# A fused attention and MoE kernel: a head pair's value products come one step later

## The chip, the cores and the metric

The kernel runs on one core of a Trainium2 chip. The metric is the device time in microseconds (us) of one execution. Engines are called as in the profile: PE (matrix products, with PEld for the loading of its weights), DVE (vector), ACT (scalar), POOL (general purpose), SP (issues transfers).

## The reference

```python
scores = scale * q @ k.T + bias          # 4 batches, 8 heads, 768 positions, head size 64
keep = is_global | is_local              # first 8 positions, or the last 96 up to the query
a = softmax(where(keep, scores, -1e9));  attn = a @ v
x = attn as 3072 tokens x 512
h = x @ w_in;  x = (h * cos(h)) @ w_out  # 512 -> 2048 -> 512
# then a top-1 mixture of 8 experts (512 -> 1024 -> 512, relu), skipped for
# tokens with x @ w_skip <= 0; the expert's output is scaled by its gate and added to x
```

All arrays are float32. Each large product is made as three products of split numbers (hi times hi, lo times hi, hi times lo).

## The kernel before, in words

The 3072 tokens are cut into 8 units of 384, that is 3 tiles of 128. A unit goes through attention and then through the first MoE (w_in, cosine, w_out). The two are woven together: while the first MoE works on unit u-1, the attention of unit u is put in between its steps. So the stretch of time of "unit 2" in what follows holds the attention of unit 2 and the MoE of unit 1.

The MoE of a unit has 16 blocks of 128 hidden columns. A block has two steps, and each ends at a slot, 32 slots a unit. In an even slot's step PE makes the 12 products `hp` (L526, input times w_in), in an odd slot's step the products `zp` (L565, activated block times w_out, two blocks behind). Round them stand the other engines' steps of the block: r on DVE (L509, L552), two ACT steps, glo on POOL (L537), and the splitting of the next weights (wi_hi on POOL L483, wi_lo on DVE L492). In unit 0's stretch DVE and POOL also convert the weights (L219, L223, L230, L264), and they are kept after that.

The attention of a unit has 4 head pairs, each 8 slots apart. A pair goes through these functions, and a table says after which slot each is written:

- `att_Tq`, `att_Tk`: transposes of q and k (PE L352, L362).
- `att_S`, once for each of 3 tiles: scores of two heads (PE L396, tile `ps_s`), and for each head one evacuation on DVE (L401) that adds the bias and takes the smallest value. Called S0, S1, S2 here.
- `att_E`: exponentials on ACT (L415), the inverse of the sums on DVE (L419, L420), and six scalings `sc` on POOL (L425).
- `att_P`, for each tile: transposes of the weights (PE L437, L440, tile `ps_p`), copied by ACT to `pT` (L441, L443). Called P0, P1, P2.
- `att_V`: the value products (PE L452, L457, tile `ps_v`). Then ACT rounds the result to `xhi` (L466), and DVE takes the rest, `xlo` (L467), both from `ps_v`. Called V.
- `att_load_va`: the loads of `ld_va`, the values of the tokens before the tile, for the next pair (one buffer).

The rows of the table (s0 is the slot of the pair's first scores; 8 slots later come those of the next pair):

```python
            for t in range(HT):
                at(s0 + t, att_S, u, p, t)
                at(s0 + 5 + t, att_P, u, p, t)
            at(s0 + 9, att_V, u, p)
            at(s0 + 2, att_load_va, u, p)
            at(s0 + 2, att_E, u, p, tail=True)
```

So V of a pair stands at the next pair's slot s0 + 1, behind its S0. The tiles `ps_s`, `ps_p`, `ps_t` and `ps_v` come in turn from one pool of three buffers in PSUM (tag "ps"); a request waits until the tile that had the buffer three requests ago has been read. The requests between two pairs' P2 were S0 (two, one for each head), V, S1 (two), S2 (two), Tq, Tk.

PE and ACT work in the order in which the code is written. On DVE, POOL and SP the order is made by a scheduler when the kernel is built.

DVE has one more kind of work that matters here. From unit 2's stretch on, `logits_v` puts the gate and skip products of an earlier unit on DVE (L623, result `junk` of 128x512, with a small read of its sum behind it): 27 in a unit, two a slot, in slots 4 to 17, so beside the first and second pairs of a unit and not beside the others. Another small piece is `cmin` (L298), a minimum over a block of w_in for a check.

Of the kernel before, what the change touches and what calls it, by code (L numbers as in the profile page):

```python
# [37 lines left out]
def kernel(  # L38
# [7 lines left out]
    NP = H // 2  # L46
# [677 lines left out]
    def at(slot, fn, *a, tail=False):  # L724
        (late if tail else ev).setdefault(slot, []).append((fn, a))
# [6 lines left out]
    for u in range(1, NU):  # L732
        for p in range(NP):
            s0 = HS * (u - 1) + PS * p - 3
            at(s0 - 12, att_load, u, p)
            at(s0 - 5, att_load_v, u, p)
            at(s0 - 5, att_Tq, u, p)
            at(s0 - 4, att_Tk, u, p)
            for t in range(HT):
                at(s0 + t, att_S, u, p, t)  # L740
                at(s0 + 5 + t, att_P, u, p, t)
            at(s0 + 9, att_V, u, p)
            at(s0 + 2, att_load_va, u, p)
            at(s0 + 2, att_E, u, p, tail=True)
    for i in range(4 * FC):
        s0 = HS + 8 + i * (HS * (NU - 2) - 24) // (4 * FC)
# [224 lines left out]
    with tc.manual_schedule(engines={mybir.EngineType.PE}):  # L971
# [8 lines left out]
        with tc.manual_schedule(engines={mybir.EngineType.SP}):  # L980
            with tc.manual_schedule(engines={mybir.EngineType.Activation}):


                u = NU - 1
# [456 lines left out]
```

## Time and profile before

| | |
|---|---|
| median of 3 runs | 1008.06 us (1006.95 to 1009.19) |
| the profiled execution | 1010.82 us |
| its span, first to last instruction | 1009.1 us |
| mean granted clock of PE | 0.979 |
| busy | PE 94%, DVE 74%, ACT 53%, POOL 53% |

The rest of this document uses views of this one profiled execution. The view of waits sums, for each engine and line, the time in which the engine stood idle, and names the instruction that ended the wait. A timeline lists instructions by start, with duration, and in brackets the idle time before one and its releaser. Busy times by stretch say how full each engine was between two times.

### The profile page before, as it was taken

The page shows a single profiled execution, that of the slowest core. Times are in us where ns is not written, and L with a number is a line of the kernel's source. Part 1 is how long each engine was busy: PE and PEld are TensorE (multiplying, and loading weights), DVE is VectorE, ACT ScalarE, POOL GpSimd, SP SyncE. Part 2 cuts the span into 40 slices and gives each one's busy share as a digit, 9 for nine tenths or more (in the row PEclk, how much of TensorE's full clock was granted, in tenths as well). Part 3 has the DMA queues.
Part 4 walks back from the last instruction along what each step waited for, and adds up shares of the span by engine and source line. Part 5 has one row for each costly group of instructions (what it writes and reads, how often), then busy time and mean ns, then how long its engine had stood idle before and what let it go on. Part 6 is the DMA issues. An engine that isn't in the chain of part 4 may idle for free.

```text
span 1009.1 us, 17130 instructions
## 1 busy us (share of the span) xinstructions
PE 953.4 (94%) x5677; PEld 803.4 (80%) x5677; DVE 751.7 (74%) x1871; ACT 535.3 (53%) x1295; POOL 532.8 (53%) x707
## 2 busy tenths in 40 slices
PE   8878899999999999999999999999999889999996
PEld 4566678878878888887888788878898779999995
DVE  6679987986796689569757955885572387888882
ACT  5768878557656665665666566656463121111110
POOL 3657765545464546545454545465462355555662
PEclk7899899999999999999999999999999999999998
DMA  7497865234433443431112112100104384666400
GB/s 188 100 231 204 244 168 184 70 91 118 129 84 99 115 120 81 121 94 31 30 43 72 29 29 51 54 15 11 39 13 182 134 319 185 209 231 227 176 19 22
DMA packets 144385, 115.08 MB, mean 114 GB/s; under 512 B 100247, under 2 KB 116631, under 8 KB 144160
## 3 DMA queue, kind: packets, MB, share of 16 engines
q1 hardware_dynamic: 141056, 107.89, 36.1%
q0 software_dynamic: 3200, 5.98, 1.6%
q8 instruction: 47, 0.77, 0.3%
q14 instruction: 50, 0.41, 0.1%
q10 hardware_dynamic: 32, 0.03, 0.0%
HBM read 97.36 MB, written 21.05 MB: 117 GB/s over the span
## 4 chain that ended last, share of the span: by engine, by line
PE 57%; DVE 26%; DMA 5%; issue 5%; ACT 4%; POOL 2%; SPq 0%; POOLq 0%; ACTq 0%; DVEq 0%
PE zp L565 14%; PE hp L526 14%; DVE junk L623 9%; PE hp L946 9%; PE zp L965 9%; DVE wi_lo L492 4%; PE ps_s L396 3%; DVE r L509 2%; DVE r L552 2%; DVE sc L401 2%; DMA ck<-in_moe_w_out_dram 1%; PE ps_p L437 1%; DVE w_in_sb L223 1%; PE ps_v L457 1%; DMA st<-in_moe_w_out_dram 1%
## 5 line engine op out<-in xcount | busy, mean ns | idle before, releaser
L537 POOL TENSOR_TENSOR glo<-r,ghi 128x384 fp32r<-128x384 f32 x115 | 133.1, 1157 | 180.0 <-ACT ghi L536 149.6
L526 PE MATMUL hp<-xhi,wi_hi 128*128 128x384 f32 x492 | 177.2, 360 | 2.1 <-DVE r L552 1.3
L526 PE MATMUL hp<-xhi,wi_lo 128*128 128x384 f32 x492 | 166.9, 339 | 0.9 <-DVE wi_lo L492 0.9
L526 PE MATMUL hp<-xlo,wi_hi 128*128 128x384 f32 x492 | 165.9, 337 | 0.0
L492 DVE TENSOR_TENSOR wi_lo<-w_in_sb,wi_hi 128x512 fp32r<-128x512 f32 x128 | 114.6, 896 | 51.6 <-PE hp L526 16.8
L623 DVE CUSTOM_DVE_ANT_0 junk<-r_zr,wrep 128x512 bf16<-128x512 f32 x162 | 140.8, 869 | 8.3 <-ACT r_zr L585 6.4
L565 PE MATMUL zp<-wo_hi,ghi 128*128 128x512 f32 x345 | 146.7, 425 | 0.0
L565 PE MATMUL zp<-wo_hi,glo 128*128 128x512 f32 x345 | 137.3, 398 | 8.3 <-POOL glo L537 8.2
L565 PE MATMUL zp<-wo_lo,ghi 128*128 128x512 f32 x345 | 136.1, 395 | 0.0
L425 POOL TENSOR_SCALAR sc<-sc,sm 128x232 f32<-128x232 f32 (+1 forms) x180 | 93.6, 541 | 61.5 <-DVE sm L420 42.3
L514 ACT ACTIVATE r<-r,halfpi 128x384 f32<-128x384 f32 x128 | 79.0, 617 | 82.1 <-DVE r L509 81.0
L536 ACT CAST ghi<-r 128x384 fp32r<-128x384 f32 x115 | 59.0, 513 | 115.4 <-DVE r L552 114.3
L526 PEld LDWEIGHTS hp<-xhi,wi_hi 128*128 128x128 f32 x492 | 93.2, 189 | 16.8 <-issue 9.3
L951 ACT ACTIVATE hh<-hp 128x256 fp32r<-128x256 f32 x64 | 24.7, 387 | 152.2 <-PE hp L946 152.2
L483 POOL TENSOR_SCALAR wi_hi<-w_in_sb 128x512 fp32r<-128x512 f32 x112 | 83.7, 748 | 37.4 <-PE hp L526 32.5
L526 PEld LDWEIGHTS hp<-xhi,wi_lo 128*128 128x128 f32 x492 | 93.1, 189 | 1.2 <-DVE wi_lo L492 1.2
L526 PEld LDWEIGHTS hp<-xlo,wi_hi 128*128 128x128 f32 x492 | 93.5, 190 | 0.2
L396 PE MATMUL ps_s<-kW,qT 64*128 64x232 f32 (+1 forms) x384 | 74.0, 405 | 18.3 <-DVE xlo L467 10.8
L565 PEld LDWEIGHTS zp<-wo_hi,glo 128*128 128x128 f32 x345 | 65.6, 190 | 25.7 <-POOL glo L537 10.8
L415 ACT ACTIVATE sc<-sc,mx 128x232 f32<-128x232 f32 (+1 forms) x180 | 83.3, 464 | 3.9 <-DVE mx L401 2.7
L884 POOL TENSOR_SCALAR w2h<-we 128x512 fp32r<-128x512 f32 x64 | 46.5, 727 | 72.7 <-PE zp L965 72.7
L552 DVE TENSOR_TENSOR r<-r,hp 128x384 f32<-128x384 f32 x112 | 61.4, 549 | 25.5 <-ACT r L514 25.0
(234 smaller groups left out, 2239.6 us busy)
## 6 DMA issues: line engine op xcount, KB each, us to landing
we<-in_moe_w_dram SPq DMA_DIRECT2D x16, 2048.0 KB
st<-in_moe_w_in_dram SPq DMA_DIRECT2D x16, 512.0 KB
st<-in_moe_w_out_dram SPq DMA_DIRECT2D x16, 512.0 KB
ck<-in_moe_w_in_dram SPq DMA_DIRECT2D x32, 256.0 KB
ck<-in_moe_w_out_dram SPq DMA_DIRECT2D x32, 256.0 KB
ld_q<-in_q_dram SPq DMA_DIRECT2D x64, 96.0 KB
ld_k<-in_k_dram SPq DMA_DIRECT2D x64, 96.0 KB
ld_v<-in_v_dram SPq DMA_DIRECT2D x64, 96.0 KB
```

The lines of the kernel that those rows point to most:

```text
L396: nc.tensor.matmul(sp[:, c0:NW], d["qT"][j * D:(j + 1) * D, t * P:(t + 1) * P], d["kW"][j * D:(j + 1) * D, t, c0:NW], start=True, stop=True,)
L415: nc.scalar.activation(out=s[:, j, c0:NW], in_=s[:, j, c0:NW], func=AF.Exp, scale=-1.0, bias=d["m"][:, t, j:j + 1], accum_out=sm[:, t, j:j ...
L425: nc.gpsimd.tensor_scalar(out=s[:, j, c0:NW], in0=s[:, j, c0:NW], scalar1=sm[:, t, j:j + 1], scalar2=1.0, op0=ALU.mult, op1=ALU.mult,)
L483: nc.gpsimd.tensor_scalar(out=hi, in0=ws, scalar1=1.0, scalar2=1.0, op0=ALU.mult, op1=ALU.mult)
L492: nc.vector.tensor_tensor(out=lo, in0=ws, in1=hi.bitcast(F32), op=ALU.subtract)
L526: nc.tensor.matmul(hp, a[:, c, :], b[:, c, :], start=(n == 0), stop=(n == 3 * CC - 1))
L537: nc.gpsimd.tensor_tensor(out=glo, in0=r, in1=ghi.bitcast(F32), op=ALU.subtract)
L552: nc.vector.tensor_tensor(out=r, in0=r, in1=hp, op=ALU.mult)
L565: nc.tensor.matmul(zt[u][t], a[:, sl], b[:, f, :], start=(f == 0 and n == 0), stop=(f == FC - 1 and n == 2),)
L623: nc.vector.tensor_tensor_reduce(out=junk, in0=self.zr[:, t, 0:DM], in1=self.wrep[e], op0=ALU.mult, op1=ALU.add, scale=1.0, scalar=0.0, ac ...
L946: nc.tensor.matmul(hp, a[:, c, :], b[:, c, :], start=(n == 0), stop=(n == 3 * CC - 1))
L965: nc.tensor.matmul(yq[e][j], a[:, sl], b, start=(f == 0 and n == 0), stop=(f == F2C - 1 and n == 2),)
```

## The change

V of a pair goes from its slot s0 + 9 to s0 + 11, except for the last pair of a unit, where it stays. The load of `ld_va` goes along from s0 + 2 to s0 + 4, for all pairs. In the table are units 1 to 7, so 21 of 28 value products move. Behind the move lie the next pair's S1, one block of `zp`, its S2 and one block of `hp`.

```diff
-            at(s0 + 9, att_V, u, p)
-            at(s0 + 2, att_load_va, u, p)
+            at(s0 + (9 if p == NP - 1 else 11), att_V, u, p)
+            at(s0 + 4, att_load_va, u, p)
```

On PE, in unit 2 at its second pair's V, before the change (the last `hp` products of the slot, V, the third pair's S1, and the first `zp`):

```order
L526 MATMUL hp<-xhi,wi_lo 128x384
L457 MATMUL ps_v<-pT,ld_v 64x128 x2
L452 MATMUL ps_v<-pT,ld_va 64x128 x2
L457 MATMUL ps_v<-pT,ld_v 64x128 x2
L452 MATMUL ps_v<-pT,ld_va 64x128 x2
L457 MATMUL ps_v<-pT,ld_v 64x128 x2
L396 MATMUL ps_s<-kW,qT 128x232 x2
L565 MATMUL zp<-wo_hi,ghi 128x512
```

Of the change, the same products two slots later on (the last `hp` of that slot, V, and the transposes of q for the fourth pair):

```order
L526 MATMUL hp<-xhi,wi_lo 128x384
L457 MATMUL ps_v<-pT,ld_v 64x128 x2
L452 MATMUL ps_v<-pT,ld_va 64x128 x2
L457 MATMUL ps_v<-pT,ld_v 64x128 x2
L452 MATMUL ps_v<-pT,ld_va 64x128 x2
L457 MATMUL ps_v<-pT,ld_v 64x128 x2
L352 MATMUL ps_t<-ident,ld_q 128x128 x3
```

V now stands behind S1 and S2, so that the third pair's S0, S1 and S2 follow each other in the pool with no V between them. The requests of the pool are now S0 (two), S1 (two), S2 (two), V, Tq, Tk.

On DVE, at the same place before the change, from the last part of S0's evacuation (L401, 128x1) to the first of S1's (L401, 128x232):

```order
L401 ISA mx 128x1
L623 ISA junk,r_lg<-r_zr,wrep 128x512
L623 ISA r_lg 128x1
L623 ISA junk,r_lg<-r_zr,wrep 128x512
L623 ISA r_lg 128x1
L492 TENSOR_TENSOR wi_lo<-w_in_sb,wi_hi 128x512
L509 SCALAR_TENSOR_TENSOR r<-r,hp 128x384
L623 ISA junk,r_lg<-r_zr,wrep 128x512
L623 ISA r_lg 128x1
L467 TENSOR_TENSOR xlo<-ps_v,xhi 128x384
L401 ISA sc,mx<-ps_s,bias_n 128x232
```

And of the change:

```order
L401 ISA mx 128x1
L623 ISA junk,r_lg<-r_zr,wrep 128x512
L623 ISA r_lg 128x1
L298 TENSOR_REDUCE cmin<-ck 128x1
L623 ISA junk,r_lg<-r_zr,wrep 128x512
L623 ISA r_lg 128x1
L492 TENSOR_TENSOR wi_lo<-w_in_sb,wi_hi 128x512
L509 SCALAR_TENSOR_TENSOR r<-r,hp 128x384
L401 ISA sc,mx<-ps_s,bias_n 128x232
```

One `junk` with its read, and `xlo`, are gone from between the two evacuations. One `cmin` that stood ahead of S0's evacuation before stands between them now. Both orders put the moved `junk` behind S1's evacuations.

On DVE in unit 0's stretch, while the weights are converted, ahead of the inverse of the sums of a pair (L419, L420), before the change (the first row is the end of S2's last evacuation):

```order
L401 ISA mx 128x1
L223 SCALAR_TENSOR_TENSOR w_in_sb<-st,w_in_sb 128x4x128
L492 TENSOR_TENSOR wi_lo<-w_in_sb,wi_hi 128x512
L219 TENSOR_SCALAR w_in_sb<-st 128x4x128
L223 SCALAR_TENSOR_TENSOR w_in_sb<-st,w_in_sb 128x4x128
L419 TENSOR_SCALAR sm<-sm 128x6
L420 RECIPROCAL sm<-sm 128x6
```

And of the change:

```order
L401 ISA mx 128x1
L219 TENSOR_SCALAR w_in_sb<-st 128x4x128
L492 TENSOR_TENSOR wi_lo<-w_in_sb,wi_hi 128x512
L223 SCALAR_TENSOR_TENSOR w_in_sb<-st,w_in_sb 128x4x128
L219 TENSOR_SCALAR w_in_sb<-st 128x4x128
L223 SCALAR_TENSOR_TENSOR w_in_sb<-st,w_in_sb 128x4x128
L219 TENSOR_SCALAR w_in_sb<-st 128x4x128
L223 SCALAR_TENSOR_TENSOR w_in_sb<-st,w_in_sb 128x4x128
L419 TENSOR_SCALAR sm<-sm 128x6
L420 RECIPROCAL sm<-sm 128x6
```

The conversion rows came closer to the sums: three pairs of L219 and L223 stand between S2's evacuation and L419, where there was one and the second half of another. Some of them stood ahead of that evacuation before.

## Rows read from the trace of the kernel before

**Rows 1.** The page's first part: busy time, share of the span and instructions by engine.

```profile
PE 953.4 (94%) x5677; PEld 803.4 (80%) x5677; DVE 751.7 (74%) x1871; ACT 535.3 (53%) x1295; POOL 532.8 (53%) x707
```

**Rows 2.** Waits of the whole span: engine, waiter <- releaser: us, times, longest.

```profile
PE ps_s L396 <- DVE xlo L467: 10.8, 12, 1.5
PE zp L565 <- POOL glo L537: 8.2, 3, 3.2
```

**Rows 3.** The same view from 160 to 720 us (units 2 to 7).

```profile
PE ps_s L396 <- DVE xlo L467: 9.8, 11, 1.5
PE ps_p L437 <- POOL sc L425: 2.7, 6, 0.5
```

**Rows 4.** Windows: length, busy us of PE, PEld, DVE, ACT, POOL; clock, DMA share, GB/s.

```profile
172.56:216.77 44.21, 42.39 (x245) 35.46 (x244) 43.11 (x124) 26.07 (x64) 20.58 (x27) 0.96 0.33 91
265.69:310.25 44.56, 42.30 (x256) 34.55 (x255) 42.98 (x124) 26.80 (x65) 23.94 (x29) 1.00 0.37 102
```

**Rows 5.** Timeline, unit 2, second pair's V: start, us, engine, line, instruction, [idle before].

```profile
201.33 0.44 PE L457 MATMUL ps_v<-pT,ld_v 128*64 128x128 f32 x4
...
202.12 0.28 DVE L401 CUSTOM_DVE_ANT_0 sc<-ps_s,bias_f 128x128 f32<-128x128 f32 x1
202.33 0.68 DVE L623 CUSTOM_DVE_ANT_0 junk<-r_zr,wrep 128x512 bf16<-128x512 f32 x1
...
202.58 0.66 PE L396 MATMUL ps_s<-kW,qT 64*128 64x232 f32 x4
202.67 1.21 POOL L537 TENSOR_TENSOR glo<-r,ghi 128x384 fp32r<-128x384 f32 x1 [3.11 <-PE ps_v L457]
...
203.05 1.38 DVE L623 CUSTOM_DVE_ANT_0 junk<-r_zr,wrep 128x512 bf16<-128x512 f32 x1
...
204.36 1.09 DVE L492 TENSOR_TENSOR wi_lo<-w_in_sb,wi_hi 128x512 fp32r<-128x512 f32 x1
...
205.37 0.54 DVE L509 SCALAR_TENSOR_TENSOR r<-r,hp 128x384 f32<-128x384 int32 x1
205.84 0.68 DVE L623 CUSTOM_DVE_ANT_0 junk<-r_zr,wrep 128x512 bf16<-128x512 f32 x1
...
206.45 0.55 DVE L467 TENSOR_TENSOR xlo<-ps_v,xhi 128x384 fp32r<-128x384 f32 x1
206.92 0.38 DVE L401 CUSTOM_DVE_ANT_0 sc<-ps_s,bias_n 128x232 f32<-128x232 f32 x1
...
207.05 0.97 PE L396 MATMUL ps_s<-kW,qT 64*128 64x232 f32 x4 [1.53 <-DVE xlo L467]
```

**Rows 6.** Timeline of PE, unit 3, second pair's V.

```profile
295.95 0.44 PE L452 MATMUL ps_v<-pT,ld_va 104*64 104x128 f32 x4
...
297.42 0.66 PE L396 MATMUL ps_s<-kW,qT 64*128 64x232 f32 x4
...
301.67 0.97 PE L396 MATMUL ps_s<-kW,qT 64*128 64x232 f32 x4 [1.32 <-DVE xlo L467]
```

**Rows 7.** One tile, 172 to 311 us: ns min/median/max of its instruction.

```profile
L492 DVE TENSOR_TENSOR wi_lo<-w_in_sb,wi_hi x23: 678/705/1487, 174.7 to 306.4; 128x512 fp32r<-128x512 f32 x23
```

**Rows 8.** Windows round two stretches at half clock, as in rows 4.

```profile
205.00:208.50 3.50, 1.97 (x10) 1.23 (x9) 3.50 (x11) 0.98 (x2) 0.00 (x0) 1.00 0.25 56
208.50:211.91 3.41, 3.41 (x13) 3.32 (x12) 3.38 (x12) 3.38 (x11) 1.44 (x2) 0.50 0.28 82
577.00:580.55 3.55, 2.24 (x11) 1.55 (x10) 3.52 (x13) 1.37 (x3) 0.12 (x1) 1.00 0.24 54
580.55:583.96 3.41, 3.41 (x14) 3.22 (x13) 3.13 (x16) 3.40 (x12) 2.04 (x2) 0.50 0.00 0
```

**Rows 9.** Timelines of unit 0's stretch: one pair's sums and scalings.

```profile
84.16 4.18 POOL L425 TENSOR_SCALAR sc<-sc,sm 128x232 f32<-128x232 f32 x6 [1.52 <-ACT qT L356]
84.30 0.59 DVE L219 TENSOR_SCALAR w_in_sb<-st 128x512 int32<-128x512 int32 x1
84.93 0.82 DVE L223 SCALAR_TENSOR_TENSOR w_in_sb<-st,w_in_sb 128x512 int32<-128x512 int32 x1
...
88.31 1.16 POOL L537 TENSOR_TENSOR glo<-r,ghi 128x384 fp32r<-128x384 f32 x1
...
89.52 0.80 PE L565 MATMUL zp<-wo_hi,glo 128*128 128x512 f32 x1 [3.24 <-POOL glo L537]
```

**Rows 10.** Timeline of POOL, the same stretch, two pairs later.

```profile
142.00 2.64 POOL L425 TENSOR_SCALAR sc<-sc,sm 128x232 f32<-128x232 f32 x6 [0.54 <-DVE sm L420]
```

## The prediction

> **What bounds the kernel now.** The first view to read is the page's list of busy times: PE works 94% of the span [rows 1], so a change in the order of work can only move PE's idle time and its clock. The view of waits says what that idle time is made of. The largest item is PE waiting to write a score tile until DVE has made `xlo`: 10.8 us in 12 waits [rows 2], 9.8 us in 11 of them in units 2 to 7 [rows 3]. Next come 8.2 us in three waits of `zp` for `glo`, all in unit 0's stretch, and 2.7 us in units 2 to 7 in which the transposes of P0 wait for the scalings on POOL [rows 2, 3].
>
> Then the stretches in which the `xlo` waits lie. In the first halves of units 2 and 3, DVE is busy 43.11 of 44.21 us and 42.98 of 44.56 us [rows 4]. So in these halves DVE is as full as PE, and a DVE result comes late because of the queue ahead of it, not because its input is late. The timeline shows it [rows 5]: V begins on PE at 201.33 and S1 at 202.58, but `xlo` starts at 206.45, behind two `junk`, a `wi_lo`, an `r` and one more `junk`. S2's products start at 207.05 after 1.53 us of idling, since `ps_v` has the buffer that they need.
>
> One more thing is to be seen in this row. S2 for both heads takes 0.97 us where S1 took 0.66. Its second product needs the buffer of S1's first evacuation, which starts only at 206.92, right behind `xlo`. So S2 waits for DVE twice, with a few tenths of a microsecond between the two.
>
> **What the change removes.** With V behind S2, the buffer of S2's first product is that of S0's second evacuation, done 4.7 us earlier (it starts at 202.12 [rows 5]). The wait for `xlo` is gone by its name. S2's second product still needs S1's first evacuation, as before. The question is when that evacuation comes, against PE's arrival.
>
> PE arrives earlier, by the time of V: 202.58 - 201.33 = 1.25 us in unit 2 [rows 5], and 297.42 - 295.95 = 1.47 us in unit 3, which has 12 products instead of 10 [rows 6]. The even units are like unit 2, the odd ones like unit 3. The evacuation comes earlier by what DVE no longer does ahead of it, call that D. The time to S2's end thus changes by -D, while V's 1.25 or 1.47 us are still to come after it. The sum at one place is V minus D: a loss if D is smaller.
>
> D is read from the new DVE order, with durations from start to start of the old rows [rows 5]: the last `junk` ahead of `xlo` 0.61 (205.84 to 206.45), `xlo` 0.47 (to 206.92), another `junk` 0.72 (202.33 to 203.05). The second pair's V decides in each unit, since behind it come only places without `junk`. What is won or lost at the first pair, and at P0's waits for POOL between the two, happens ahead of it: a PE that comes there earlier or later meets the same DVE queue.
>
> - Units 2 and 6: one `junk` and `xlo` leave, D = 1.08. Each place +0.17.
> - Unit 3: the same, +0.39.
> - Unit 4: the same and one `cmin` leave (about 0.33), but one `wi_lo` comes in. It costs between 0.6 (a median one of 705 ns [rows 7] less its overlap with the next) and 1.0 (204.36 to 205.37 [rows 5]). So +0.45 to +0.85; I take +0.6.
> - Units 5 and 7: two `junk` and `xlo` leave, D = 1.80. Each -0.33.
>
> The sum of six is 2 x 0.17 + 0.39 + 0.6 - 2 x 0.33 = +0.7 us. That V now stands ahead of Tq costs nothing by itself: V takes the buffer of S1's second evacuation and Tq that of S2's first, while a block of 12 `hp` products lies between S2 and V. The third pair's V, in all units, moves between work with no `junk` and no waits: 0. The exponentials on ACT come ahead of `xhi`, and P1 of the next pair waits for `xlo`, but P0 waits for POOL's scalings anyway, which come later. The loads of `ld_va` follow V by one slot as before, and on SP's queue they pass the issues of two slots; I cost this at nothing, as V comes 6 slots after them. Were they late, PE would wait for them at V; nothing in the old trace gives a price for that, and I leave it out of the range.
>
> **Unit 0's stretch.** Here the weights are converted, and the order shows that DVE now does an additional L219 and L223 pair between S2's evacuation and the sums L419, 0.63 + 0.82 = 1.4 us (84.30 to 84.93, and the duration [rows 9]), and `xlo`, 0.47, no longer. So the sums come 0.9 us later at two pairs. Behind the sums stand POOL's six scalings (4.18 us), then `glo` (88.31), for which PE idles 3.24 us until 89.52 [rows 9]. This is the chain that sets the end there, so a late sum is a late `zp`. Against that, the scalings ran beside DVE's conversions; two pairs later the same six took 2.64 us [rows 10]. With fewer conversions left to run beside them, they may win back up to 1.5 us. I take +0.3 for each of two pairs, between -0.1 and +0.9; +0.6 in all.
>
> A rule speaks on this: the Trainium skill, page "SBUF — State Buffer", section "Who interferes with whom", says that a DVE operation with two SBUF inputs and GpSimd reading SBUF shut each other out of a shared port pair, the second one blocked outright. The rows agree in kind: the `junk` at 203.05 took 1.38 us while POOL's `glo` ran from 202.67 to 203.88, and the one at 205.84 took 0.68 [rows 5] in a window in which POOL did nothing [rows 8].
>
> **The clock.** PE's granted clock fell to 0.50 for 3.41 us at 208.50, right after the 1.53 us wait, and again at 580.55 after a window with PE busy 2.24 of 3.55 us [rows 8]. Of 3.41 us at half clock, half is lost, about 1.7 us each. Other waits of over 1.2 us, as the 1.32 us of unit 3 [rows 6], had no fall behind them (the window of unit 3 shows 1.00 [rows 4]). The waits stay near what they were, so I keep both falls: 0. Bounds: both go (-3.4), or three more come (+5.1).
>
> **Sum.** +0.7 and +0.6 make +1.3 us on the profiled span, 1009.1 to 1010.4, and on its time, 1010.82 to 1012.1. That execution was 2.76 us above the median of its runs, so for the median I add the same: 1008.06 + 1.3 = **1009.3 us**. About 0.2%, or 2.0 us, is what a measurement can tell from no change here.
>
> **The rivals.**
>
> *A, the whole gain.* S1's first evacuation comes early enough, and PE waits for DVE no more: the 10.8 us go [rows 2], with both falls of the clock (3.4): 1008.06 - 14.2 = 994. For it speaks that the named wait can't exist any more; against it that DVE has no gap in these stretches [rows 4] and the next wait follows within tenths of a microsecond [rows 5].
>
> *B, a part of it.* The `junk` that leaves the place is of the slow kind (1.38 us beside POOL [rows 5]), so D = 1.38 + 0.47 = 1.85, and every place wins 0.4 to 0.6 us: 3 x (1.25 - 1.85) + 3 x (1.47 - 1.85) = -2.9. Shorter waits spare the two falls, -3.4, and unit 0 costs +0.6: 1002.4. The skill's rule above would bear this out where POOL works beside that `junk`; but POOL is idle at 205.84 [rows 8].
>
> *C, slower by the clock.* This is the case on the other side. S1's second product now needs S0's first evacuation, and PE gets there 1.25 us sooner: 201.64 or so, against an end of that evacuation near 202.2 [rows 5]. So a wait of half a microsecond or more stands at S1, ahead of S2's own wait a few microseconds later. Two idle pieces close together are what stood ahead of the falls at 208.50 and 580.55 [rows 8]. It decides if three more of twelve places fall: 3 x 1.7 + 1.3 = +6.4, so 1014.5. Against it: most waits of this size had none. The Trainium skill, page "TensorE: Matmul & The Clock Gate", section "A second HAM failure mode: psum-queue depth-cycling", describes this: small idle pieces from cycling through few PSUM buffers bring the clock down again and again. The rows bear out two falls in units 2 to 7.
>
> *D, slower by unit 0.* The scalings get no faster, and both `zp` come 0.9 us later: +1.8 in place of +0.6, so 1010.5, just over the bound.
>
> **How the numbers follow.** Forecast (within 2.0 us of 1008.06) 0.38; A 0.10; B 0.14; C 0.20; D 0.18. Faster are A and B, 0.24; same 0.38; slower C and D, 0.38. The range from 1002 to 1014 leaves out A and the upper half of C, 0.2 together. It holds the bounds of unit 4 (0.2 each way), of unit 0 (-0.8 to +1.2) and the loss of both falls.
>
> **What would show it.** In the changed kernel's waits, `ps_s` no longer waits for `xlo`, but for the evacuations (L401) with a like sum, at S2 and in small pieces at S1. DVE stays without gaps in the stretches of [rows 4]. P0's waits for POOL shrink in units 2 to 7. In unit 0's stretch `zp` still waits for `glo` by about 3 us or more. I am wrong if the `ps_s` waits sum to under 6 us, which means that DVE gets ahead (A, B), or if the windows at 0.50 are more than those before by three (C).

## The result, and the profile after

The change made the kernel slower: 1013.7 us against 1007.4 us (medians of 14 runs each). One of the 14 runs of the change took 1306.49 us at a granted clock of 0.649, and the ratio leaves it out: 1.0054 with a 95% interval of 1.0041 to 1.0067. That is +5.4 us (+4.1 to +6.8); the two medians lie 6.3 us apart. The forecast was 1009.3 us, with a range of 1002 to 1014. The measured median lies in the range, near its upper end, and on the side of the rivals C and D. The case behind the forecast, no measurable change, did not come about.

The profiled execution after took 1015.5 us with a span of 1013.7, against 1010.82 and 1009.1 before. In its view of waits for units 2 to 7 (as [rows 3]: engine, waiter <- releaser: us, times, longest):

```profile
PE ps_s L396 <- DVE mx L401: 9.7, 11, 1.7
PE ps_s L396 <- DVE xlo L467: 0.8, 1, 0.8
PE ps_p L437 <- POOL sc L425: 0.3, 1, 0.3
```

Before, [rows 3] had 9.8 us for `xlo` and 2.7 us for the scalings. So the named wait is gone, but for one place, and in this view a wait for the score evacuations has taken its place at the same size. The waits of P0 for POOL are all but gone.

The sums in this view are too small. Here is the timeline of PE in unit 7, at the scores of the third pair, before:

```profile
668.91 0.77 PE L396 MATMUL ps_s<-kW,qT 64*128 64x232 f32 x4
...
673.20 0.97 PE L396 MATMUL ps_s<-kW,qT 64*128 64x232 f32 x4 [1.23 <-DVE xlo L467]
```

And after:

```profile
669.09 0.66 PE L396 MATMUL ps_s<-kW,qT 64*128 64x232 f32 x2
671.46 0.66 PE L396 MATMUL ps_s<-kW,qT 64*128 64x232 f32 x2 [1.72 <-DVE mx L401]
...
674.32 0.66 PE L396 MATMUL ps_s<-kW,qT 64*128 64x232 f32 x2
675.60 0.66 PE L396 MATMUL ps_s<-kW,qT 64*128 64x232 f32 x2 [0.63 <-DVE mx L401]
```

Before, the first row is S1 and the second S2, each with both heads' products in one row (x4). S2 waits once ahead of the row, and its second product some 0.3 us more inside it (0.97 us in place of 0.66). After, both tiles have come apart into two rows (x2), one for each head, and both second products wait. S1's second product starts 2.37 us after the first (671.46 - 669.09). In places without a wait the two heads' products start together, 0.01 us apart, and both take 0.66 us in all. So it waited 2.36 us, of which the row shows 1.72; the rest is hidden in the 0.66 us that the first row is drawn as busy. Counted in this way, from start to start, the waits of the scores between the two marks below are 16.3 us before and 22.2 after.

DVE's timeline between them shows why (only its longer instructions; the rows of 0.08 us that read a sum are left out):

```profile
670.54 0.55 DVE L552 TENSOR_TENSOR r<-r,hp 128x384 f32<-128x384 f32 x1
671.01 0.39 DVE L401 CUSTOM_DVE_ANT_0 sc<-ps_s,bias_n 128x232 f32<-128x232 f32 x1
...
671.33 0.39 DVE L401 CUSTOM_DVE_ANT_0 sc<-ps_s,bias_n 128x232 f32<-128x232 f32 x1
...
671.64 0.69 DVE L623 CUSTOM_DVE_ANT_0 junk<-r_zr,wrep 128x512 bf16<-128x512 f32 x1
...
672.37 1.37 DVE L623 CUSTOM_DVE_ANT_0 junk<-r_zr,wrep 128x512 bf16<-128x512 f32 x1
...
673.68 1.08 DVE L492 TENSOR_TENSOR wi_lo<-w_in_sb,wi_hi 128x512 fp32r<-128x512 f32 x1
674.69 0.54 DVE L509 SCALAR_TENSOR_TENSOR r<-r,hp 128x384 f32<-128x384 int32 x1
675.15 0.38 DVE L401 CUSTOM_DVE_ANT_0 sc<-ps_s,bias_n 128x232 f32<-128x232 f32 x1
```

S0's first evacuation ends at 671.40, and S1's second product starts at 671.46. S1's first evacuation ends at 675.53, and S2's second product starts at 675.60. Both products want a buffer that DVE has not read yet, and DVE has no gap, as in [rows 4].

Two marks bound the stretch in which V was moved beside `junk`: the first scores of unit 2's first pair and those of unit 7's fourth pair. On PE after:

```profile
153.34 0.48 PE L396 MATMUL ps_s<-kW,qT 64*128 64x128 f32 x2
...
692.46 0.66 PE L396 MATMUL ps_s<-kW,qT 64*128 64x232 f32 x4
```

Before, these stood at:

```profile
152.51 0.49 PE L396 MATMUL ps_s<-kW,qT 64*128 64x128 f32 x2
...
688.76 0.66 PE L396 MATMUL ps_s<-kW,qT 64*128 64x232 f32 x4
```

The stretch grew from 536.25 to 539.12 us, by 2.87. The rest of the span's 4.6 us lies outside: 0.83 ahead of it, 0.9 behind it.

Half clock, at last. In this stretch the clock after was at 0.50 in two pieces of 3.41 us, as many as before [rows 8], but at other places:

```profile
298.30:301.71 3.41, 3.41 (x9) 2.26 (x7) 3.41 (x9) 0.56 (x1) 1.82 (x2) 0.50 0.26 79
486.03:489.44 3.41, 3.41 (x9) 2.71 (x9) 3.38 (x7) 0.18 (x2) 2.20 (x2) 0.50 0.00 0
```

### The profile page after: what moved, and what is told of

The parts are those of the page before. It is cut to its first block, busy times and chain, and to the rows that moved or that the text cites. A ratio compares the mean times of both kernels' runs of the same rounds, so it can differ in the third digit from the quotient of the medians.

```text
span 1013.7 us, 17170 instructions
## 1 busy us (share of the span) xinstructions
PE 957.8 (94%) x5673; PEld 803.2 (79%) x5677; DVE 755.5 (75%) x1871; ACT 535.5 (53%) x1295; POOL 532.0 (52%) x707
## 4 chain that ended last, share of the span: by engine, by line
PE 57%; DVE 19%; issue 3%; ACT 2%; DMA 2%; POOL 1%; POOLq 0%; ACTq 0%; DVEq 0%
PE zp L565 16%; PE hp L526 14%; PE hp L946 9%; PE zp L965 9%; DVE junk L623 8%; DVE wi_lo L492 3%; PE ps_s L396 3%; DVE r L509 2%; DVE r L552 2%; PE ps_v L457 1%; PE ps_v L452 1%; DMA ck<-in_moe_w_in_dram 1%; DVE sc L401 1%; PE ps_p L437 1%; PE ps_t L352 1%
## 5 line engine op out<-in xcount | busy, mean ns | idle before, releaser
L492 DVE TENSOR_TENSOR wi_lo<-w_in_sb,wi_hi 128x512 fp32r<-128x512 f32 x128 | 120.8, 944 | 52.9 <-PE hp L526 17.4
L623 DVE CUSTOM_DVE_ANT_0 junk<-r_zr,wrep 128x512 bf16<-128x512 f32 x162 | 137.8, 851 | 8.4 <-ACT r_zr L585 6.3
L425 POOL TENSOR_SCALAR sc<-sc,sm 128x232 f32<-128x232 f32 (+1 forms) x180 | 89.7, 520 | 62.7 <-DVE sm L420 43.0
L483 POOL TENSOR_SCALAR wi_hi<-w_in_sb 128x512 fp32r<-128x512 f32 x112 | 88.3, 789 | 33.6 <-PE hp L526 30.0
L396 PE MATMUL ps_s<-kW,qT 64*128 64x232 f32 (+1 forms) x384 | 78.2, 405 | 14.5 <-DVE mx L401 12.6
L498 ACT ACTIVATE r<-hp 128x384 int32<-128x384 f32 x123 | 60.2, 489 | 39.2 <-PE hp L526 34.8
```

The lines of the kernel that those rows point to most:

```text
L396: nc.tensor.matmul(sp[:, c0:NW], d["qT"][j * D:(j + 1) * D, t * P:(t + 1) * P], d["kW"][j * D:(j + 1) * D, t, c0:NW], start=True, stop=True,)
L425: nc.gpsimd.tensor_scalar(out=s[:, j, c0:NW], in0=s[:, j, c0:NW], scalar1=sm[:, t, j:j + 1], scalar2=1.0, op0=ALU.mult, op1=ALU.mult,)
L483: nc.gpsimd.tensor_scalar(out=hi, in0=ws, scalar1=1.0, scalar2=1.0, op0=ALU.mult, op1=ALU.mult)
L492: nc.vector.tensor_tensor(out=lo, in0=ws, in1=hi.bitcast(F32), op=ALU.subtract)
L623: nc.vector.tensor_tensor_reduce(out=junk, in0=self.zr[:, t, 0:DM], in1=self.wrep[e], op0=ALU.mult, op1=ALU.add, scale=1.0, scalar=0.0, ac ...
```

## The experiments

Three theories stood against each other. The *queue theory*: S1 and S2 wait for evacuations behind a full DVE queue, and V's time comes on top. The *clock theory*: the new waits bring more stretches at half clock. The *unit-0 theory*: the late sums in unit 0's stretch cost. The other runs ask which of the moved V cost, and what takes the waits away. Ratios are to the kernel before, on the same chip, with 95% intervals. All diffs are to the kernel after, if nothing else is said.

**The loads alone.**

```diff
-            at(s0 + (9 if p == NP - 1 else 11), att_V, u, p)
+            at(s0 + 9, att_V, u, p)
```

> Only the loads of ld_va go from s0+2 to s0+4; every V stays at s0+9. Load theory (the other issue order on SP, or later loads, makes the cost): most of the measured +5.4 us, ratio 1.004 to 1.005. Queue theory, clock theory and unit-0 theory: no change, 1.000 within 0.002, the xlo waits at S2 as before (about 10 us).

Measured: 1.0000 (0.9982 to 1.0019). No cost of the loads is to be seen, and the load theory falls.

**Unit 1 alone.**

```diff
-            at(s0 + (9 if p == NP - 1 else 11), att_V, u, p)
+            at(s0 + (11 if u == 1 and p < NP - 1 else 9), att_V, u, p)
```

> V moves only for unit 1's first three pairs, that is in unit 0's stretch, beside the conversion of the weights. Unit-0 theory (later sums, later scalings, later zp): +1.2 to +3 us, ratio 1.001 to 1.003, and it makes up much of the cost. Queue theory and clock theory: at most +0.3 to +0.6 us, 1.000 to 1.001; the xlo waits of units 2 to 7 stay as before.

Measured: 0.9990 (0.9968 to 1.0013). A loss of over 0.13% in unit 0's stretch is outside the interval, so the unit-0 theory does not carry the cost.

**The second pair alone.**

```diff
-            at(s0 + (9 if p == NP - 1 else 11), att_V, u, p)
+            at(s0 + (11 if u > 1 and p == 1 else 9), att_V, u, p)
```

> V moves only for the second pair of units 2 to 7 (six places). Queue theory: S1's and S2's second products wait for the evacuations, V's own time less the DVE work taken from ahead costs +0.7 to +1.3 us in all, ratio 1.001. Clock theory: the waits at S1 and S2 bring one to three more half-clock stretches of 1.7 us on average, 1.003 to 1.005. If the second pair does not matter: 1.000.

Measured: 1.0015 (0.9993 to 1.0037). That fits the queue theory, but the interval holds no change as well, and the lower end of the clock theory. The waits at S1 and S2 are there:

```profile
PE ps_s L396 <- DVE mx L401: 3.4, 6, 1.0
PE ps_s L396 <- DVE xlo L467: 2.5, 4, 1.5
```

The clock speaks against the clock theory here: over these 12 runs the mean granted clock was 0.9768, against 0.9737 before on the same chip. Time at half clock loses half of itself, so this alone would make the runs some 3.0 us shorter; they were 1.3 us longer in the mean. By this estimate the second pair's move costs about 4 us of other time, which the higher clock hides.

**The first and third pairs.**

```diff
-            at(s0 + (9 if p == NP - 1 else 11), att_V, u, p)
+            at(s0 + (11 if u > 1 and p in (0, 2) else 9), att_V, u, p)
```

> V moves only for the first and third pairs of units 2 to 7 (twelve places). Queue theory: PE gains at the first pair, and gives it back at the second pair's S2, which waits for xlo longer by as much: 1.000 within 0.001. Clock theory: these longer waits bring some more half-clock stretches, 1.001 to 1.003. A real gain, if the first pair's gain is kept: 0.995 to 0.997.

Measured: 1.0036 (1.0015 to 1.0057), over the queue theory's bound. This was the surprise: pairs at which I had put no cost make a good part of it. The next two kernels take them apart.

**The first pair alone.**

```diff
-            at(s0 + (9 if p == NP - 1 else 11), att_V, u, p)
+            at(s0 + (11 if u > 1 and p == 0 else 9), att_V, u, p)
```

> V moves only for the first pair of units 2 to 7 (six places). In the run with first and third pairs PE gained 0.3 to 2.5 us at the first pair and gave it back, with new half-clock stretches, at the second. Give-back theory: all of that run's cost is here, ratio 1.003 to 1.004, S2 of the second-next pair waiting for xlo longer (well over 12 us in sum) and one to three half-clock stretches more than the two of before in units 2 to 7. If the third pair makes the cost: 1.000.

Measured: 1.0064 (1.0043 to 1.0085), as much as the whole change or more. V of the second pair stands in its old place here, and the wait is again the one for `xlo` at the third pair's S2. The timeline of PE at four of the six places:

```profile
303.13 0.97 PE L396 MATMUL ps_s<-kW,qT 64*128 64x232 f32 x4 [1.86 <-DVE xlo L467]
...
396.33 0.97 PE L396 MATMUL ps_s<-kW,qT 64*128 64x232 f32 x4 [1.64 <-DVE xlo L467]
...
491.37 0.97 PE L396 MATMUL ps_s<-kW,qT 64*128 64x232 f32 x4 [2.38 <-DVE xlo L467]
...
679.85 1.03 PE L396 MATMUL ps_s<-kW,qT 64*128 64x232 f32 x4 [2.37 <-DVE xlo L467]
```

At unit 3 it was 1.32 us before [rows 6]. And behind each of the six places the clock fell in the profiled execution; the windows of this kernel (columns as in [rows 4]):

```profile
209.59:213.00 3.41, 3.41 (x13) 3.31 (x12) 3.32 (x13) 3.38 (x11) 1.33 (x2) 0.50 0.27 82
305.16:308.57 3.41, 3.41 (x13) 3.18 (x12) 3.38 (x16) 3.40 (x12) 2.65 (x4) 0.50 0.00 0
397.31:400.72 3.41, 3.41 (x11) 3.41 (x12) 3.33 (x15) 3.28 (x9) 1.01 (x1) 0.50 0.27 77
492.88:496.29 3.41, 3.41 (x15) 3.31 (x13) 1.67 (x10) 3.38 (x11) 1.81 (x4) 0.50 0.00 0
585.05:588.46 3.41, 3.41 (x11) 2.82 (x11) 3.41 (x13) 2.59 (x7) 1.01 (x1) 0.50 0.00 0
680.62:684.03 3.41, 3.41 (x12) 3.22 (x11) 2.20 (x14) 3.07 (x7) 1.36 (x3) 0.50 0.00 0
```

Six where there were two: four more at 1.7 us are 6.8 us, and the stretch between the two marks grew by 7.0. Six is the count of this execution, which was the slowest of its six runs (1017.76 us) with the lowest granted clock, 0.964; the others had 0.969 to 0.976. Over all six the clock was 0.9703, against 0.9749 before on the same chip. By the same estimate as for the second pair, the clock accounts for 4.8 us of the 7.1 us between the means of the runs.

**The third pair alone.**

```diff
-            at(s0 + (9 if p == NP - 1 else 11), att_V, u, p)
+            at(s0 + (11 if u > 1 and p == 2 else 9), att_V, u, p)
```

> V moves only for the third pair of units 2 to 7, where there is no junk on DVE. Queue, clock and give-back theories: nothing to win or lose, 1.000 within 0.002, waits as before. Third-pair theory (the next pair's P0 or P1 or the fourth pair's scores come late): 1.003.

Measured: 1.0011 (0.9996 to 1.0026). No cost to be seen there; the third-pair theory falls.

The marks and waits of these kernels side by side, from one profiled execution each. The waits are added up from the starts of products between the two marks: idle time ahead of a score tile's first product, and what the second head's product starts more than 0.01 us after the first's. "1st" to "3rd" are the scores of the first to third pairs (the fourth pair's have at most 0.1). "P" is what the groups of transposes (P0, P1, P2) took longer, from the start of the product ahead of them to that of the one behind, than the median of groups with the same neighbours in these eight kernels. Falls are stretches of 3.41 us at half clock.

```
V moved in units 2-7 at   marks apart   change    1st   2nd    3rd     P    sum   falls
none (before)               536.25        0       1.4   4.9   10.0   4.9   21.2     2
none (loads only)           534.42       -1.8     1.4   4.5   10.0   4.9   20.9     1
none (unit 1 only)          536.64       +0.4     1.5   3.8   10.0   4.8   20.1     3
third pair                  536.15       -0.1     2.2   3.5   10.4   4.3   20.4     2
second pair                 536.21        0.0     2.8   4.5   10.3   4.6   22.2     1
first and third             539.97       +3.7     1.1   2.8   17.1   0.0   21.0     4
first pair                  543.29       +7.0     1.5   2.8   17.4   0.0   21.6     6
all three (after)           539.12       +2.9     2.2   4.6   15.4   0.6   22.8     2
```

Take 1.7 us per fall off, relative to before, and what remains is, from the second row on, -0.1, -1.3, -0.1, +1.7, +0.3, +0.2 and +2.9. The sum of the waits changes by -0.3, -1.1, -0.8, +1.0, -0.2, +0.4 and +1.6, so the two together account for each stretch to within 0.8 us, and for the full change to within 1.3. Moving the first pair's V shifts the waiting from the second pair's scores, and from P, to the third pair's: 17.4 us there in place of 10.0, while the sum hardly changes. What it costs in these executions are the falls behind the longer waits. Moving the second pair's V costs more waiting and not more falls; the time of its own runs does not tell this from no change.

**Scores of both heads in one bank, V in its old place** (diff to the kernel before).

```diff
+        sp2 = ps_a.tile([P, 2, 256], F32, name="ps_s", tag="ps")
         for j in range(2):
-            sp = ps_a.tile([P, 512], F32, name="ps_s", tag="ps")
+            sp = sp2[:, j]
```

> V as before the change, but the scores of both heads of a tile share one PSUM bank, so an S takes one buffer of the pool and not two; S2 then needs the buffer of S0, read long before. Buffer theory (the waits are for a free buffer, and DVE's queue only makes them long): the ps_s waits for xlo go (9.8 us), with the half-clock stretches behind them; faster, ratio 0.988 to 0.995. DVE-bound theory (DVE has no gap in these stretches, so PE only meets another late DVE result): ps_s waits go, other waits on DVE (r, wi_lo) take their place, 0.998 to 1.001.

Measured: 1.1223 (1.1184 to 1.1262). Neither theory: the edit made a new wait within every tile. The timeline of this kernel at an S1 (its L397 is PE's score line, its L402 the evacuation):

```profile
204.46 0.66 PE L397 MATMUL ps_s<-kW,qT 64*128 64x232 f32 x2
...
205.34 0.39 DVE L402 CUSTOM_DVE_ANT_0 sc<-ps_s,bias_n 128x232 f32<-128x232 f32 x1
...
205.79 0.66 PE L397 MATMUL ps_s<-kW,qT 64*128 64x232 f32 x2 [0.68 <-DVE mx L402]
```

The second head's product, in the same bank, waits until DVE has read the first head's. Over the whole span these waits sum to 80.3 us in 86 places. The Trainium skill, page "TensorEngine Tiling (Array Packing)", section "Gotcha 1: PSUM Pressure", says that products from different row halves of the array can't use one bank at the same time, and that the software has to order them; the two heads lie in different halves. Whether the order seen here comes from this, or only from the two heads sharing one tile, no run shows. A form with both products ahead of both evacuations wasn't tried. So this pair of kernels says nothing on buffers.

**The same with V moved.** The same edit on the kernel after.

> The change with the same one-bank scores. Buffer theory: without the shortage of buffers it does not matter where V stands, so the ratio is that of V in its old place with one-bank scores, within 0.002, and the new waits of S1 and S2 for the evacuations (L401) are gone. Rival: V's late xlo or the changed DVE order costs by itself, then 0.003 to 0.005 above V in its old place.

Measured: 1.1698 (1.1645 to 1.1752), with 86.8 us of that wait. For the same reason it decides nothing.

**Gate and skip products on PE, V in its old place** (diff to the kernel before; the buffer for the DVE products' weights is left out as well).

```diff
-        if u + 2 < NU:
+        if u < 0:
```

> V as before the change; the gate and skip products of all units are made on PE, as the last two units' are, so the junk leaves DVE. Backlog theory: no xlo wait of note at S2 (under 2 us in sum in units 2 to 7) and no half-clock stretch there. PE pays for it: the rows of the one unit that makes them on PE in these stretches sum to about 3.6 us, times six is 21 us, less some 7 us of waits and 3.4 us of half clock: ratio 1.008 to 1.013. If the waits do not come from the junk they stay, and the ratio is 1.02.

Measured: 1.0289 (1.0256 to 1.0323). The waits of `ps_s` are gone, as expected, but the gate products on PE wait instead:

```profile
PE ps_l L615 <- ACT zT L610: 8.4, 3, 3.1
PE ps_l L615 <- ACT kW L371: 5.8, 3, 1.9
```

Half clock did not go, against the expectation: the clock stood at 0.50 in six pieces between the marks, one in each unit from 2 to 7, of 3.41 us four times and 6.83 us twice. By 1.7 us for each 3.41 us that is about 13.6 us more, beside 14.2 us of waits. The mean granted clock of the runs was 0.9672, against 0.9753 before on the same chip.

**The same with V moved.** The same edit on the kernel after.

> The change with the same products on PE. Backlog theory: without the backlog on DVE it does not matter where V stands: within 0.002 of the same kernel with V in its old place. Rival (V's new place costs by itself, as by the pool or by xlo's lateness for the next pair): 0.003 to 0.006 above it.

Measured: 1.0037 (1.0018 to 1.0055). Here the view of waits of PE has no row at all between 160 and 720 us, and no half clock there. Two windows of it, units 2 and 3 (columns as in [rows 4]):

```profile
172.00:216.00 44.00, 44.00 (x282) 37.22 (x281) 26.95 (x88) 28.64 (x70) 16.63 (x28) 1.00 0.39 114
264.00:310.00 46.00, 46.00 (x299) 38.89 (x298) 27.07 (x85) 30.18 (x73) 18.30 (x31) 1.00 0.38 110
```

DVE is busy 27 us instead of 43, and the waits of S1 and S2 are zero, as they are with V in its old place: without the backlog of `junk` they do not come. One reservation is that the edit also gives PE more work (282 products in a stretch where it had 245 [rows 4]), so that PE arrives later too. My comparison failed, though: I expected the two V places to be alike without the backlog, and the new place is 2.5% faster here. The old one has waits of `ps_l` for ACT and half clock behind them, 14.2 and about 13.6 us, and the new one has neither; the two spans differ by 29.1 us (1037.2 and 1008.1). So in these kernels V's place has no value of its own; it depends on the work around it. Why ACT is late for `ps_l` I did not follow up.

**Four wi_lo of a unit on POOL, V in its old place** (diff to the kernel before).

```diff
-            split_lo((f + 1) % FC)
+            side_ = 1 <= u <= 6 and f in (3, 5, 7, 9)
+            split_lo((f + 1) % FC, eng=nc.gpsimd if side_ else nc.vector)
```

> V as before the change; four of the sixteen wi_lo of units 1 to 6 (those in the stretch with junk) are made on POOL instead of DVE, about 3 to 4 us less for DVE in each first half. Backlog theory: S2's waits for xlo of 1.2 to 1.5 us shrink to under 0.5, the two half-clock stretches go: ratio 0.990 to 0.996. Rival: POOL's longer queue makes the scalings or glo late, or POOL and DVE slow each other: 1.000 to 1.005.

Measured: 1.0164 (1.0138 to 1.0189). The rival's side, and by more than it said. The scalings on POOL came late, as it had said; before, this wait was 2.7 us in 6 places [rows 3]:

```profile
PE ps_p L437 <- POOL sc L425: 8.2, 9, 1.7
```

Counted as in the table, P grew from 4.9 to 11.3 us and all waits from 21.2 to 33.1, with one fall more; the marks moved apart by 13.1 us. And DVE gained little: the group of `junk` of this kernel, for which the old mean from 172 us on was 869 ns:

```profile
L623 DVE CUSTOM_DVE_ANT_0 junk<-r_zr,wrep 128x512 bf16<-128x512 f32 x162 | 153.4, 947 | 8.8 <-ACT r_zr L585 6.4
```

**The same with V moved.** The same edit on the kernel after.

> The change with the same four wi_lo on POOL. Backlog theory: the waits of S1 and S2 for L401 shrink as well, and the difference to V in its old place falls from 0.5% to under 0.2%. Rival as for the other: 1.005 or more.

Measured: 1.0196 (1.0169 to 1.0223), so 0.3% above the old place. The two intervals just overlap. With seven falls between the marks where the old place has three, and waits of 29.7 us in place of 33.1, it shows the same two costs, waits and falls, but the backlog was not taken away, so the test of the theory fell through. No version was faster than the kernel before by more than its interval.

## Why the prediction was right or wrong

**Right: the wait is replaced.** S2's wait for `xlo` went and the waits for the evacuations came, at S2's second product as the working said, and at S1's second product as rival C said. DVE stayed without gaps (busy 42.64 of 43.80 us and 43.35 of 45.00 in the first halves of units 2 and 3). P0's waits for POOL shrank from 2.7 to 0.3 us. Rival A had nothing to stand on, and rival B's faster evacuations did not come. That 1013.7 us lies inside the range owes something to luck: the upper end was there for half of rival C, more falls of the clock, and the profiled execution of the change has none more between the marks.

**Too small: the sum of V minus D.** The six places were to cost +0.7 us. In the profiled execution the two marks moved apart by 2.9 us at an equal number of falls, with 1.6 us more of waits. Of this, 1.3 us lies between the first scores of the second and of the fourth pair in the six units together, so the sum of D was off by a factor of two; 0.8 us is the one wait for `xlo` left, at unit 3's first pair, where the fourth pair's V of unit 2 had kept its place and which the working left out; the rest is small pieces. One reading in the working was off: rival C's 201.64 us for S1's second product takes it as 0.3 us behind the first, but the two start together (202.58 [rows 5]), so it comes to 201.33, and the wait there is 0.3 us longer than the working has it.

**Wrong: what happens at the first pair is absorbed.** The prediction said that a PE that comes earlier "meets the same DVE queue", so the first pair counted for nothing. The meeting is as said: what the second pair's scores and P save, 7.0 us, is given back at the third pair's scores, 7.4 us. But it is given back as a longer wait, and the runs put a price on that. With the first pair's V alone, the waits at the third pair's scores rose from 10.0 to 17.4 us and the falls from two to six in the profiled execution; over its runs the clock fell from 0.9749 to 0.9703 and the time rose by 0.64%. "I keep both falls: 0" was the term that failed there.

**Rival C, in part.** Its price per fall, 1.7 us, and its mechanism of a second wait at S1 are borne out. For the full change the falls are not. They are two against two in the profiled executions. Over the timed runs the mean granted clock was 0.9741 for the change, against 0.9737, 0.9749 and 0.9753 for the kernel before in the three sets of runs of the experiments. The first pair alone shows it in the timed runs: 0.9703 against 0.9749 on the same chip. The second pair alone goes the other way, 0.9768 against 0.9737. So the full change may hold both, one against the other; that is no more than a suspicion, as no run shows the sum. Why a wait of 2.36 us, as at unit 7, has no fall behind it in the full change, where the first-pair kernel had one behind 2.37 us of idling at the same pair, is open.

**Near in size, not in its steps: unit 0.** In the rows after, the scalings took 3.75 us, not 4.18, and `zp` resumed at 89.86 instead of 89.52:

```profile
84.66 3.75 POOL L425 TENSOR_SCALAR sc<-sc,sm 128x232 f32<-128x232 f32 x6 [2.12 <-DVE sm L420]
...
89.86 0.80 PE L565 MATMUL zp<-wo_hi,glo 128*128 128x512 f32 x1 [3.23 <-POOL glo L537]
```

That looks like the +0.3 that I had put [rows 9], but this pair's rows do not show it. `zp` waited as long as before (3.23 and 3.24 us), and PE was 0.5 us behind before any V had moved: the first `hp` product stands at 50.37 us before and at 50.87 after. The sums L419 are later by no more than that, 83.57 and 84.07. At the second pair `zp` resumed at 119.90 instead of 118.72. To the first mark the whole stretch lost 0.83 us in this execution, the 0.5 included; some 0.3 is left for the two pairs together, where the working had +0.6. The working also counted an additional L219 and L223 where the two orders differ by two L219 and one L223. Rival D, +1.8 us here, falls with the run of unit 1 alone, whose interval ends at 1.0013. That the loads cost nothing was right (1.0000).

**What stays open.** The stretch between the marks explains 2.9 us of the measured 5.4 (4.1 to 6.8). The 1.7 us outside the marks in the profiled execution are of the size by which other kernels differ there: the first mark stands between 1.3 us earlier and 1.7 us later than before in the six kernels that move V or the loads in part, and the time behind the second mark is 320.3 us before, 321.2 after and 318.3 to 320.2 in those six. What the other runs of the change spent the rest on, no profile here tells. Nor is V's place on PE told apart from the order on DVE: the scheduler makes that order anew for each kernel, and no run holds it fixed.

## What to carry to other kernels

Here a wait that was taken away, on an engine whose releaser had a full queue, came back at the next thing that the queue held. Work out where it comes back, and how long it is there, not only the sum. Idle time that is merely moved can cost more in its new place: in the first-pair kernel, idle pieces that grew from about 1.3 to about 2 us had half-clock stretches behind them. Moving one part of a change at a time shows this, where the whole hides it in the sum.

## What was not expected of the hardware

Moving six V products by two slots, with next to no change in the sum of idle time (21.2 and 21.6 us), cost 0.64%. In the profiled execution almost all of it was four more stretches of 3.41 us at half clock; over the runs the clock makes about two thirds of it. The idle pieces that had a fall behind them in the first-pair run were 1.53 to 2.38 us long; before, pieces of 1.31 and 1.53 us had one, and those of 1.32, 1.25, 1.24 and 1.23 had none. And `junk` on DVE went from 869 to 947 ns in the mean when POOL took over four weight splits a unit, which ate 12.6 us (153.4 against 140.8 in sum) of the some 21 us that these (24 of 0.87 us) had freed. The rule of the Trainium skill that the prediction named, page "SBUF — State Buffer", section "Who interferes with whom", is of this kind; the rows agree in direction. Between kernels that leave POOL's work alone the mean of `junk` also varies, from 848 to 869 ns, which is less than this step.
